# Moving both copies of each sorted tile to ScalarE, and the small loads ahead of the large ones, in a linear-attention and mixture-of-experts kernel

## The chip, the cores and the metric

The kernel runs on one core of a Trainium2 chip. The metric is the device time of one execution in microseconds. Before the change it is 276.43 us, the median of 3 runs that lie between 275.39 and 279.25 us. Engines are named as the profile names them: PE is TensorE (PEld its weight loads), DVE is VectorE, ACT is ScalarE, POOL is GpSimd, SP is SyncE, which here issues the loads.

## The reference

Eight batches of 576 tokens go through a linear attention with 8 heads of 64, and the 4608 rows of 512 that come out go through a mixture of experts in which each token takes its one best expert.

```python
def _attn_ref(q, k, v):                      # (8, 8, 576, 64) each
    q_s = softmax(q, axis=-1)                # over the head dimension
    k_s = softmax(k, axis=2)                 # over the sequence
    kv = np.einsum('bhsd,bhse->bhde', k_s, v)
    return np.einsum('bhsd,bhde->bhse', q_s, kv)

def _moe_ref(x, modality_id, w_gate, modality_bias, w1, w2):   # x (4608, 512)
    logits = x @ w_gate + modality_bias[modality_id]           # 8 experts
    e_idx = np.argmax(logits, axis=1)
    gate_w = softmax(logits)[arange, e_idx]
    for e in range(8):
        mask = e_idx == e
        h = np.maximum(x[mask] @ w1[e], 0.0)                   # 512 -> 1024
        out[mask] = gate_w[mask, None] * (h @ w2[e])           # 1024 -> 512
    return out
```

With the biases of this problem nearly every token goes to one of two experts, one for each modality. The kernel finds these two from the bias table and sorts every batch's tokens by them: tokens of expert A fill the buffer `xs` from the left, those of expert B from the right. It then runs the feed-forward network (FFN) of A over the left part and of B over the right part. A loop at the end serves tokens of other experts. It is skipped if there are none.

## The kernel before

Each batch goes through `prep` (exponentials of k and q on ACT, cast of v), `attend` (attention and gate logits, on PE and DVE) and `route`. `route` picks the expert of each token, builds a permutation `perm` for each of five tiles of tokens (64, then four times 128), scales the attention rows (`scale`), permutes and transposes them on PE (`xT_ps`) and copies each tile into `xs` twice. Copy "a" goes to the left end that expert A has reached, and copy "b" to the right end of B. The rows of the other expert are overwritten by the next tile's copies. Where a copy lands is known only on chip: the copying engine loads the five offsets from `aoff_i` into registers.

```python
        scale(0)
        na = ...; pos = ...                                    # DVE, small
        perm = sb.tile([P, NT, P], BF16, name="perm")
        nc.vector.tensor_tensor(out=perm, in0=iota_row..., in1=pos..., op=ALU.is_equal)
        at = {}
        for side, eng in (("a", ENG.Activation), ("b", ENG.DVE)):
            at[side] = nc.values_load_multi_w_load_instructions(aoff_i[0:1, o : o + NT], engines=[eng], ...)[1]
        yield 3
        scale(1)
        for t in range(NT):
            xT_ps = (ka if b else ff).tile([P, KD, P], FP32, name="xT_ps", ...)
            for kd in range(KD):
                nc.tensor.matmul(out=xT_ps[:, kd, 0:T], lhsT=x_out[t]..., rhs=perm[0:T, t, 0:T], ...)
            if t + 2 < NT:
                xps.append(x_tile(b, t + 2))                   # PE: attention rows of tile t+2
            for side, off, eng in (("a", 0, nc.scalar), ("b", right, nc.vector)):
                a = nc.s_assert_within(at[side][t], ...)
                copy_on(eng, window(a + off, b, T, off > 0), xT_ps[:, :, 0:T], ...)
            yield 1
            if t + 2 < NT:
                scale(t + 2)
```

PSUM pools: `ka` has 2 banks (for `kv_ps`, `tp_ps`, `kvT_ps`, and `xT_ps` after batch 0), `mm` 2 (`x_ps`), `ff` 3 (`h_ps`, `y_ps`), `sp_ps` 1.

The FFN is cut into pieces. One piece of `ffn1` is 8 matmuls of 128x256 into an `h_ps` and a relu on ACT into `hT`; four of them make a pass of 256 tokens. One piece of `ffn2` is 4 matmuls of 128x512 into a `y_ps`, and after every second piece comes the copy to `y_sb` and an indirect store. The copies alternate between DVE and ACT:

```python
            y_sb = ybuf.tile([P, D], FP32, name="y_sb")
            copy_on(nc.scalar if t else nc.vector, y_sb, y_ps)
            store = nc.gpsimd.indirect_dma_start(out=out, ..., in_=y_sb, ...)
```

Instruction order on every engine is fixed by the program: a piece is issued where `weave` calls it. A `yield x` in `attend` or `route` stands for x times `rate` pieces of the FFN of earlier batches:

```python
    def weave(side, rate, preps=(), first=0):
        owed = 0.0
        for i, x in enumerate(side):
            if i >= first:
                next(preps, None)          # ACT exponentials and POOL casts of the next batch
            owed += x * rate
            while owed >= 1:
                mains(1)
                owed -= 1
    ...
    for b in range(2, B):                  # batches 2 to 7
        weave(batch(b), 16 / 24.3, prep(b + 1, nc.gpsimd) if b + 1 < B else (), 4)
```

Batches 0 and 1 are placed by hand ahead of that loop, with the casts of the two experts' weights between them. What is left of the FFN after batch 7 runs at the end, alone. At the start SP issues the loads of batch 0 (k, v, q, 1152 KB each), then the gate weights and the modality ids, then batch 1. The bias table is loaded by POOL's queue. POOL converts the ids (`mbf`) and the gate weights (`wgb`), and POOL and DVE clear two of the four parts of `xs` each.

Of the kernel before, what the change touches and what calls it, by code (L numbers as in the profile page):

```python
# [11 lines left out]
FP32 = mybir.dt.float32  # L12
BF16 = mybir.dt.bfloat16
I32 = mybir.dt.int32
# [6 lines left out]
P = 128  # L21
# [21 lines left out]
def kernel(  # L43
# [67 lines left out]
    def load_batch(b, names="kvq", eng=nc.sync):  # L111
# [13 lines left out]

    load_batch(0)
    bias_1 = const.tile([1, 2, E], FP32)
    nc.gpsimd.dma_start(
        out=bias_1,
# [5 lines left out]
    for hl in range(2):  # L135
# [13 lines left out]
        out=mraw, in_=bass.AP(tensor=m32.tensor, offset=m32.offset, ap=[[2 * S, B], [1, 2 * S]])  # L149
    )  # L150
    load_batch(1)


    ident = const.tile([P, P], BF16)
    make_identity(nc, ident)
# [17 lines left out]
    )  # L173
    iota_i = const.tile([P, E], I32)
    nc.gpsimd.iota(iota_i, pattern=[[1, E]], base=0, channel_multiplier=0)
    wrow = const.tile([P, E], FP32)
# [6 lines left out]
    for hg in range(2):  # L183
# [3 lines left out]
    idh_i = const.tile([P, B, NT], I32)  # L187
    nc.vector.tensor_scalar(out=idh_i, in0=id_i, scalar1=7, scalar2=None, op0=ALU.logical_shift_right)
    idl_i = const.tile([P, B, NT], I32)
    nc.vector.tensor_scalar(out=idl_i, in0=id_i, scalar1=127, scalar2=None, op0=ALU.bitwise_and)  # L190

    vals = const.tile([P, B, NT, 3], BF16)
    nc.vector.tensor_copy(out=vals[:, :, :, 0], in_=idh_i)
    nc.vector.tensor_copy(out=vals[:, :, :, 1], in_=idl_i)

# [15 lines left out]
    mbf = const.tile([B, NJ, 64], BF16)  # L211
    nc.gpsimd.tensor_copy(out=mbf, in_=view(mraw, [[2, NJ], [2 * NJ, 64]]))
    wgb = ybuf.tile([P, D], FP32, name="y_sb").bitcast(BF16)
    nc.gpsimd.tensor_copy(
        out=view(wgb, [[2 * Dh, E], [1, 2 * Dh]], 0, (0, NP)),
# [3 lines left out]
    xs = persist.tile([P, KD, NSLOT], BF16)  # L219
    xs_w = [  # L220
        (nc.vector, nc.gpsimd)[kd % 2].memset(xs[:, kd, :].bitcast(FP32), 0.0) for kd in range(KD)
    ]
    lst = persist.tile([P, 3, NSL], FP32)
# [117 lines left out]

    def copy_on(eng, out, in_, then=lambda w: None):
        then((nc.scalar.copy if eng is nc.scalar else eng.tensor_copy)(out=out, in_=in_))  # L343

# [23 lines left out]
    def attend(b):  # L368
# [58 lines left out]
        nc.scalar.copy(out=kvT, in_=kvT_ps[:, 0 : NP * P])  # L427
        yield 2.3
        g_ps = sp_ps.tile([P, NP, E], FP32, name="g_ps", tag="sp")
# [48 lines left out]

    lws, qis, last_w, ids = {}, {}, {}, {}
    FIRST = [next(x for x in passes if x[0] == ph and x[1] == 0) for ph in range(NPH)]  # L480
# [29 lines left out]
    def route(b):  # L510
# [22 lines left out]
        xps.append(x_tile(b, 1))  # L533
        yield 1.5
        r_ps = sp_ps.tile([P, 2, NT], FP32, name="r_ps", tag="sp")
# [38 lines left out]
        )  # L574
        at = {}
        for side, eng in (("a", ENG.Activation), ("b", ENG.DVE)):
            at[side] = nc.values_load_multi_w_load_instructions(
                aoff_i[0:1, o : o + NT],
                engines=[eng],
                min_val=0,  # L580
                max_val=N - P,
                skip_runtime_bounds_check_because=WHY,
            )[1]
        yield 3
        scale(1)
        for t in range(NT):
            T = tsz[t]
            xT_ps = (ka if b else ff).tile([P, KD, P], FP32, name="xT_ps", tag="ka" if b else "ff")
            for kd in range(KD):
                nc.tensor.matmul(  # L590
                    out=xT_ps[:, kd, 0:T],
                    lhsT=x_out[t][0:T, kd * P : (kd + 1) * P],
                    rhs=perm[0:T, t, 0:T],
                    start=True,
                    stop=True,
                )
            if t + 2 < NT:
                xps.append(x_tile(b, t + 2))
            right = NSLOT - (b * S + cum[t])
            for side, off, eng in (("a", 0, nc.scalar), ("b", right, nc.vector)):  # L600
                a = nc.s_assert_within(at[side][t], 0, b * S + cum[t] - T, skip_runtime_bounds_check_because=WHY)
                copy_on(eng, window(a + off, b, T, off > 0), xT_ps[:, :, 0:T], lambda w: written(w, side))
            yield 1
            if t + 2 < NT:
                scale(t + 2)

        nc.vector.tensor_copy(out=vals[:, b, :, 2], in_=kk)
# [25 lines left out]
        ids[b] = (hlo, hv)  # L633
        yield 1

# [31 lines left out]
    stored = []  # L667

    def ffn1(lo, w, slot, hT):

        nf = 512 // w
        for f0 in range(0, KF, nf):
            h_ps = ff.tile([P, 512], FP32, name="h_ps", tag="ff")
            for f in range(nf):
                for kd in range(KD):
                    nc.tensor.matmul(  # L676
                        out=h_ps[:, f * w : (f + 1) * w],
                        lhsT=W[:, slot, kd * F + (f0 + f) * P : kd * F + (f0 + f + 1) * P],
                        rhs=xs[:, kd, lo : lo + w],
                        start=(kd == 0),  # L680
                        stop=(kd == KD - 1),
                    )
            nc.scalar.activation(  # L683
                out=hT[:, f0 : f0 + nf, 0:w], in_=view(h_ps, [[w, nf], [1, w]]), func=ACT.Relu
            )
            yield

    def ffn2(w, slot, hT, ix, stores):
        for t in range(w // P):
# [11 lines left out]
            y_sb = ybuf.tile([P, D], FP32, name="y_sb")  # L701
            copy_on(nc.scalar if t else nc.vector, y_sb, y_ps)
            store = nc.gpsimd.indirect_dma_start(  # L703
# [31 lines left out]

    def mains(n):
        for _ in range(n):
            next(main, None)
            now[0] += 1

# [13 lines left out]
    def alone(*sides):  # L754
        for side in sides:
            for _ in side:
                pass
# [6 lines left out]
    gating()  # L764
    p0, p1 = prep(0, nc.vector), prep(1, nc.gpsimd)
    alone(p0)
    eids = nc.values_load_multi_w_load_instructions(
# [4 lines left out]
    for b in range(2, B):  # L772
        load_batch(b)
    a0, a1, r0, r1 = attend(0), attend(1), route(0), route(1)
    for _ in range(6):
        next(a0)
    gate_weights()
    next(a0)
    biases()
    next(a0)  # L780
    next(p1)
    next(p1)
    alone(a0)
    next(p1)
    next(p1)
    next(r0)
    next(r0)
    alone(p1)
    cast_weights(0, 0, nc.gpsimd)
    cast_weights(0, 1, nc.scalar)  # L790
    for _ in range(3):
        next(a1)
    next(r0)

    for _ in range(4):
        next(r0)
        next(a1)
    cast_weights(0, 2, nc.gpsimd)
    alone(r0)
    cast_weights(0, 3, nc.scalar)  # L800
    mains(1)
# [9 lines left out]
    cast_weights(1, 2, nc.gpsimd)  # L811
    weave(r1, 0.4)
    cast_weights(1, 3, nc.scalar)
    mains(8 - now[0])
# [15 lines left out]
    for b in range(2, B):  # L830
        weave(batch(b), 16 / 24.3, prep(b + 1, nc.gpsimd) if b + 1 < B else (), 4)
    mains(3)
    places(B - 1)

    cnt = persist.tile([P, 1], FP32)
# [95 lines left out]
```

## Time and profile before

| | |
|---|---|
| median of 3 runs | 276.43 us |
| span of the profiled execution | 278.0 us |
| PE busy | 208.0 us, 75% of the span, 1994 matmuls |
| DVE, ACT, POOL busy | 63%, 46%, 31% |
| loads and stores | 46.58 MB, 168 GB/s over the span |
| first FFN matmul | at 41.99 us |
| batch 2's first attention matmul | at 72.44 us |
| last `xT_ps` matmul, batch 7 | at 219.2 us |
| last store issued | at 266.0 us |

No engine is busy all the time, so the shares alone do not say what bounds the kernel. The useful cut is by stage: the start until the first FFN piece, batch 1 with the first pieces, the six batches of the loop, the rest of the FFN, and the end after the last store. In each one asks what PE waits for, because nearly all the arithmetic is on PE, and at which clock PE ran: the profile gives the granted clock by slice and by window, and the same group of matmuls takes longer where it is low. Times in the profile are of one execution, which was a little longer than the median.

### The profile page before, as it was taken

To read this page: it belongs to the slowest core of one execution; us is meant where nothing else is said; L and a number is where in the kernel's file an instruction comes from. 1 tells how busy PE (TensorE), PEld (TensorE's weight loads), DVE (VectorE), ACT (ScalarE), POOL (GpSimd) and SP (SyncE) were. 2 spreads that over 40 slices of the span, in tenths; PEclk is the share of its full clock that TensorE was granted. 3 is DMA by queue.
4 is the path that set the end of the run, shared out by engine and by line. 5 is a ranking of instruction groups with operands and counts; after the bars stand their busy time and mean duration, and the time that the engine had idled before them with its cause. 6 is when DMAs were issued, how large, how long until landed. Compare 5 with 4: busy or idle time off the path is not lost. (4 is left out here: it accounts for less than half of the span.)

```text
span 278.0 us, 5316 instructions
## 1 busy us (share of the span) xinstructions
PE 208.0 (75%) x1994; PEld 143.7 (52%) x1994; DVE 174.1 (63%) x540; ACT 128.1 (46%) x194; POOL 86.3 (31%) x94
## 2 busy tenths in 40 slices
PE   0075189479997899788878968878897969999910
PEld 0064166246764476465646544646574646666500
DVE  4877886965448677884987778586958761111200
ACT  2333645136974476457638453744152424444200
POOL 6099206014251134151216114320312042222220
PEclk9999999856999799999999999997998899999985
DMA  6999999951999407827731011110012012112200
GB/s 242 369 392 402 398 394 367 365 197 42 361 393 403 168 20 261 325 80 250 254 121 40 38 39 41 40 48 28 2 75 77 2 53 78 73 75 78 93 15 1
DMA packets 19002, 46.58 MB, mean 168 GB/s; under 512 B 1291, under 2 KB 1291, under 8 KB 18972
## 3 DMA queue, kind: packets, MB, share of 16 engines
q1 hardware_dynamic: 15900, 36.76, 36.2%
q0 software_dynamic: 3072, 9.44, 9.0%
q8 instruction: 17, 0.28, 0.4%
q14 instruction: 13, 0.11, 0.1%
HBM read 36.75 MB, written 9.96 MB: 168 GB/s over the span
## 5 line engine op out<-in xcount | busy, mean ns | idle before, releaser
L676 PE MATMUL h_ps<-xs,W 128*128 128x256 bf16 (+1 forms) x640 | 79.7, 278 | 2.7 <-ACT xs L343 2.2
L703 POOL DMA_INDIRECT out_dram<-y_sb,ix x38 | 38.2, 1004 | 132.0 <-DVE y_sb L343 48.3
L692 PE MATMUL y_ps<-W,hT 128*128 128x512 bf16 x304 | 76.8, 391 | 0.0
L676 PEld LDWEIGHTS <-W 128*128 128x128 bf16 x640 | 60.1, 101 | 14.0 <-issue 3.8
L683 ACT ACTIVATE hT<-h_ps 128x512 bf16<-128x512 f32 x76 | 44.7, 599 | 25.2 <-PE h_ps L676 23.0
L692 PEld LDWEIGHTS <-hT 128*128 128x128 bf16 x304 | 27.9, 100 | 27.2 <-issue 3.0
L343 DVE COPY y_sb<-y_ps 128x512 f32<-128x512 f32 x20 | 13.8, 688 | 37.0 <-PE y_ps L692 35.4
L343 ACT CAST xs<-xT_ps 128x512 f32 (+2 forms) x40 | 21.9, 548 | 31.8 <-PE xT_ps L590 31.7
L590 PE MATMUL xT_ps<-perm,x_sb 128*128 128x128 bf16 (+1 forms) x160 | 17.3, 243 | 24.0 <-DVE perm L572 12.9
L343 DVE CAST xs<-xT_ps 128x512 f32 (+2 forms) x40 | 25.5, 637 | 12.8 <-ACT xs L343 12.3
L343 ACT COPY y_sb<-y_ps 128x512 f32<-128x512 f32 x18 | 10.5, 584 | 44.6 <-PE y_ps L692 40.8
L590 PEld LDWEIGHTS <-x_sb 128*128 128x128 bf16 (+1 forms) x160 | 12.3, 111 | 32.3 <-DVE x_sb L558 18.5
L558 DVE TENSOR_TENSOR x_sb<-x_ps,qi 128x512 bf16<-128x512 f32 (+1 forms) x40 | 27.2, 679 | 2.1 <-DVE perm L572 2.1
L623 POOL TENSOR_TENSOR hv<-hhi,vals 128x570 bf16<-128x570 bf16 x8 | 11.8, 1471 | 35.1 <-DVE hhi L619 29.8
L361 ACT ACTIVATE eq<-st 128x1152 bf16<-128x1152 f32 x16 | 18.5, 1165 | 4.5 <-DMA st<-in_q_dram 4.5
L361 ACT ACTIVATE ek<-st 128x1152 bf16<-128x1152 f32 x16 | 18.4, 1164 | 4.2 <-DMA st<-in_k_dram 4.2
L470 PE MATMUL x_ps<-kvbd,et 128*128 128x128 bf16 (+1 forms) x160 | 18.5, 248 | 0.0
L378 PE MATMUL kv_ps<-vb,ek 64*128 64x129 bf16 x288 | 12.6, 239 | 5.3 <-DVE vb L343 2.8
L343 POOL CAST vb<-st 128x1152 bf16<-128x1152 f32 x14 | 15.9, 1159 | 0.0
L378 PEld LDWEIGHTS <-ek 64*128 64x128 bf16 x288 | 10.1, 104 | 8.7 <-issue 7.4
L470 PEld LDWEIGHTS <-et 128*128 128x128 bf16 (+1 forms) x160 | 12.6, 114 | 3.7 <-issue 2.3
L411 PE MATMUL tp_ps<-ident,eq 128*128 128x128 bf16 x144 | 13.8, 242 | 0.5 <-DVE kvbd L399 0.5
(141 smaller groups left out, 212.0 us busy)
## 6 DMA issues: line engine op xcount, KB each, us to landing
st<-in_k_dram SPq DMA_DIRECT2D x8, 1152.0 KB, 7.2
st<-in_v_dram SPq DMA_DIRECT2D x8, 1152.0 KB, 7.9
st<-in_q_dram SPq DMA_DIRECT2D x8, 1152.0 KB, 8.1
st<-in_moe_w_dram SPq DMA_DIRECT2D x8, 1024.0 KB, 11.8
out_dram<-y_sb,ix POOLq DMA_INDIRECT x38, 2.7
W<-in_moe_modality_id_dram SPq DMA_DIRECT2D x1, 36.0 KB
hT<-in_moe_w_gate_dram SPq DMA_DIRECT2D x2, 8.0 KB
bias<-n_moe_modality_bias_dram POOLq DMA_DIRECT2D x1, 0.1 KB, 5.3
```

The costliest lines, as they stand in the source:

```text
L343: then((nc.scalar.copy if eng is nc.scalar else eng.tensor_copy)(out=out, in_=in_))
L361: nc.scalar.activation(out=view((eks if nm == "k" else eqs)[b], [[Dh, 2], [HG * Dh, NJ], [1, Dh]], 2 * g * Dh), in_=src[:, 2 * g : 2 * g + ...
L378: nc.tensor.matmul(out=kv[hg][:, 130 * hp : 130 * hp + 129], lhsT=ek[rows, j, P * hp : P * hp + P], rhs=vb[rows, j, hp, 0:129], start=(j = ...
L411: nc.tensor.transpose(out=view(tp, [[2 * nj * 64, 2], [1, 64]], hp * nj * 64 + jj * 64), in_=eq[:, c0 + jj, P * hp : P * hp + P], identity ...
L470: nc.tensor.matmul(out=view(x_ps, [[2 * Dh, 2], [1, Dh]], (4 * (p_ % 2) + p_ // 2) * Dh, (0, T)), lhsT=et[:, p_, tcol[t] : tcol[t] + T], r ...
L558: nc.vector.tensor_tensor(out=view(x_out[t], [[2 * Dh, HG], [Dh, 2], [1, Dh]], 0, (0, T)), in0=view(xps[t], [[2 * Dh, HG], [Dh, 2], [1, Dh ...
L590: nc.tensor.matmul(out=xT_ps[:, kd, 0:T], lhsT=x_out[t][0:T, kd * P : (kd + 1) * P], rhs=perm[0:T, t, 0:T], start=True, stop=True,)
L623: nc.gpsimd.tensor_tensor(out=hv, in0=view(hhi, [[NSL, NT], [0, 3], [1, NSL]]), in1=view(vals, [[3, NT], [1, 3], [0, NSL]], b * NT * 3), o ...
L676: nc.tensor.matmul(out=h_ps[:, f * w : (f + 1) * w], lhsT=W[:, slot, kd * F + (f0 + f) * P : kd * F + (f0 + f + 1) * P], rhs=xs[:, kd, lo ...
L683: nc.scalar.activation(out=hT[:, f0 : f0 + nf, 0:w], in_=view(h_ps, [[w, nf], [1, w]]), func=ACT.Relu)
L692: nc.tensor.matmul(out=y_ps, lhsT=hT[:, kf, t * P : (t + 1) * P], rhs=W[:, slot, W2 + kf * D : W2 + (kf + 1) * D], start=(kf == 0), stop=( ...
L703: store = nc.gpsimd.indirect_dma_start(out=out, out_offset=bass.IndirectOffsetOnAxis(ap=ix[:, t : t + 1], axis=0), in_=y_sb, in_offset=Non ...
```

## The change

The change has five parts.

1. **Sorted tile.** Both copies of a tile are on ACT. Only ACT loads the five offsets. While the tiles of a batch are sorted, a variable `free` sends relus and output copies that fall there to DVE. Outside, relus and output copies are all on ACT; in the rest of the FFN after the loop the output copies alternate as before.
2. **Small loads first.** Bias table, gate weights and ids are issued by SP ahead of batch 0; the gate weights, the biases and the token ids are made ready before batch 0's attention.
3. **POOL.** It no longer converts ids and gate weights (ACT does), and it clears all of `xs`.
4. **Weight casts.** They are spread anew: ACT casts part 0 of the first expert, DVE part 1, POOL parts 2 and 3; part 3 of the second expert goes from ACT to DVE.
5. **FFN pieces.** The weights of the yields change, above all 3 to 4.5 between `perm` and the first tile, and 1 to 1.4 for each tile, with the rate changed to 16/28.9 so that a batch still has room for 16 pieces. `mains` issues no piece that would need a batch not yet sorted.

The aim is that the chain through a batch's sort no longer alternates between ACT and DVE, that PE has pieces to do where it waited, and that batch 0 gets through sooner.

The diff, cut:

```diff
-    load_batch(0)
     bias_1 = const.tile([1, 2, E], FP32)
-    nc.gpsimd.dma_start(
+    nc.sync.dma_start(
...
+    load_batch(0)
     load_batch(1)
...
-    nc.gpsimd.tensor_copy(out=mbf, ...)
+    nc.scalar.copy(out=mbf, ...)
...
-    nc.gpsimd.tensor_copy(
+    nc.scalar.copy(
         out=view(wgb, ...
...
-    xs_w = [
-        (nc.vector, nc.gpsimd)[kd % 2].memset(xs[:, kd, :].bitcast(FP32), 0.0) for kd in range(KD)
-    ]
+    xs_w = [nc.gpsimd.memset(xs[:, kd, :].bitcast(FP32), 0.0) for kd in range(KD)]
...
         nc.scalar.copy(out=kvT, in_=kvT_ps[:, 0 : NP * P])
-        yield 2.3
+        yield 3
...
-        yield 1.5
+        yield 1.4
...
-        for side, eng in (("a", ENG.Activation), ("b", ENG.DVE)):
-            at[side] = nc.values_load_multi_w_load_instructions(...)[1]
-        yield 3
+        at = nc.values_load_multi_w_load_instructions(..., engines=[ENG.Activation], ...)[1]
+        yield 4.5
         scale(1)
+        free[0] = nc.vector
         for t in range(NT):
...
-            for side, off, eng in (("a", 0, nc.scalar), ("b", right, nc.vector)):
-                a = nc.s_assert_within(at[side][t], ...)
-                copy_on(eng, window(a + off, b, T, off > 0), xT_ps[:, :, 0:T], lambda w: written(w, side))
-            yield 1
+            for side, off in (("a", 0), ("b", right)):
+                a = nc.s_assert_within(at[t], ...)
+                written(nc.scalar.copy(out=window(a + off, b, T, off > 0), in_=xT_ps[:, :, 0:T]), side)
+            yield 1.4
...
+        free[0] = nc.scalar
...
         ids[b] = (hlo, hv)
-        yield 1
+        sorted_.append(b)
+        yield 1.5
...
-            nc.scalar.activation(out=hT..., in_=h_ps..., func=ACT.Relu)
+            if free[0] is nc.vector:
+                nc.vector.tensor_scalar_max(out=h_out, in0=h_in, scalar1=0.0)
+            else:
+                nc.scalar.activation(out=h_out, in_=h_in, func=ACT.Relu)
...
-            copy_on(nc.scalar if t else nc.vector, y_sb, y_ps)
+            copy_on(free[0] or (nc.scalar if t else nc.vector), y_sb, y_ps)
...
         for _ in range(n):
-            next(main, None)
-            now[0] += 1
+            if now[0] < 16 * len(sorted_) - 4:
+                next(main, None)
+                now[0] += 1
...
-    alone(p0)                              # batch 0's exponentials and cast, right after gating()
...
+    gate_weights()
+    biases()
+    token_ids()                            # four small DVE operations, moved from the setup
+    p0, p1 = prep(0, nc.vector), prep(1, nc.gpsimd)
     a0, a1, r0, r1 = attend(0), attend(1), route(0), route(1)
+    alone(p0)
...
-    cast_weights(0, 0, nc.gpsimd)
-    cast_weights(0, 1, nc.scalar)
+    cast_weights(0, 0, nc.scalar)
...
+    cast_weights(0, 2, nc.gpsimd)
+    cast_weights(0, 1, nc.vector)
+    cast_weights(0, 3, nc.gpsimd)
...
-    weave(r1, 0.4)
-    cast_weights(1, 3, nc.scalar)
+    weave(r1, 0.3)
+    cast_weights(1, 3, nc.vector)
...
-        weave(batch(b), 16 / 24.3, ...)
+        weave(batch(b), 16 / 28.9, ...)
     mains(3)
     places(B - 1)
+    free[0] = None
```

## The prediction

> **What bounds the kernel now.** I read the busy time by window first, with borders at the first FFN piece, the first attention matmul of batch 2, the last sorted tile and the last store. Columns: window, length, busy time of each engine (instructions), granted PE clock, DMA share, GB/s.
>
> ```profile
> 0.00:42.00 42.00, 16.90 (x200) 13.84 (x201) 32.37 (x97) 17.68 (x21) 19.37 (x34) 1.00 0.98 366
> 42.00:72.40 30.40, 23.13 (x172) 15.76 (x171) 20.49 (x61) 13.90 (x21) 11.35 (x8) 0.78 0.71 250
> 72.40:219.50 147.10, 124.77 (x1308) 86.23 (x1308) 108.77 (x333) 79.91 (x126) 40.37 (x37) 0.97 0.38 138
> 219.50:265.80 46.30, 43.24 (x318) 27.83 (x315) 12.48 (x51) 16.65 (x28) 14.25 (x14) 1.00 0.18 68
> 265.80:278.00 12.20, 0.00 (x0) 0.00 (x0) 0.00 (x0) 0.00 (x0) 0.97 (x1) 0.61 0.03 9
> ```
>
> The first stage belongs to no engine: a chain through loads, DVE and ACT. In the loop PE is busy 124.8 of 147.1 us, DVE 74%, ACT 54%, so PE is the nearest bound and its 22.3 us of idle time are what can be had. In the rest PE is nearly full. Next, PE's list of waits in the loop's window (who waited for whom, us in total, times, longest):
>
> ```profile
> PE xT_ps L590 <- DVE x_sb L558: 8.3, 10, 1.3
> PE xT_ps L590 <- DVE perm L572: 5.2, 6, 1.2
> PE g_ps L431 <- ACT kvT L427: 2.9, 5, 0.8
> PE kv_ps L378 <- DVE xs L343: 2.5, 5, 0.6
> PE h_ps L676 <- ACT xs L343: 1.3, 1, 1.3
> PE kvT_ps L425 <- ACT et L343: 0.8, 5, 0.2
> PE r_ps L536 <- DVE isa L528: 0.6, 1, 0.6
> PE tp_ps L411 <- DVE kvbd L399: 0.5, 1, 0.5
> ```
>
> These are 22.1 us, all of PE's idle time in the loop, and three quarters stand in the sort. Third, the timeline of one sort, batch 6 (DVE):
>
> ```profile
> 160.75 0.82 DVE L572 TENSOR_TENSOR perm<-iota_row,pos 128x640 bf16<-128x640 bf16 x1
> 162.38 0.69 DVE L558 TENSOR_TENSOR x_sb<-x_ps,qi 128x512 bf16<-128x512 f32 x1 [0.80 <-DVE perm L572]
> 162.99 0.41 DVE L343 CAST xs<-xT_ps 128x256 f32 x1
> 163.32 0.68 DVE L558 TENSOR_TENSOR x_sb<-x_ps,qi 128x512 bf16<-128x512 f32 x1
> 164.24 0.69 DVE L343 CAST xs<-xT_ps 128x512 f32 x1 [0.24 <-ACT xs L343]
> ```
>
> After `perm` DVE stands 0.80 us before `scale(1)`; in program order only its load of five offsets lies there. Then scales and "b" copies alternate. A "b" copy waits for the "a" copy of ACT, though both only read `xT_ps`.
>
> **What the Trainium skill says.** (1) "PSUM — Partial Sum Buffer", section "PSUM bank collisions raise a hardware error": two engines may not touch one bank and partition at once, reads included. The trace agrees: in all, 12.3 us (21 times) of DVE's idle time before `xs` copies end with ACT's `xs` copy. So copies on two engines do not run side by side; moving "b" to ACT lengthens no tile. (2) "TensorE: Matmul & The Clock Gate", section "What's actually happening": the PE clock is halved after an idle spell, and activity restores it. The trace agrees in kind: granted clock 0.50 from 56 to 65 us, after a wait of 3.15 us; there 4 FFN matmuls take 1.91 us, at full clock 1.03. (3) "SBUF — State Buffer", section "Who interferes with whom": a DVE instruction with two SBUF inputs is held up by a GpSimd one that reads SBUF. The trace agrees: `perm` of batch 0 beside a POOL weight cast takes 2.46 us, the median 0.83.
>
> ```profile
> 30.98 1.90 POOL L343 CAST W<-st 128x2048 bf16<-128x2048 f32 x1 [3.57 <-DMA st<-in_moe_w_dram]
> 31.09 2.46 DVE L572 TENSOR_TENSOR perm<-iota_row,pos 128x640 bf16<-128x640 bf16 x1
> ```
>
> **Part by part.**
>
> *The loop, engines.* Per batch DVE loses five "b" copies: 4 x 0.69 + 0.42 = 3.2 us (rows by shape), and the 0.8 us at the offsets. ACT gains the same copies at its own rate: 4 x 0.59 + 0.37 = 2.7 us. In the program's order per batch two output copies fall into the sort, so they stay two on DVE and two on ACT, and nearly all 8 relus stay on ACT. ACT per batch: exponentials 4 x 1.16 = 4.7, et 1.0, kvT 0.6, relus 8 x 0.6 = 4.8, outputs 2 x 0.58 = 1.2, copies 2 x 2.7 = 5.5, sum 17.8, with the offset load about 19 us. DVE: 108.8 / 6 = 18.1 - 3.2 = 15 us. PE: in the loop 124.8 us, less about 2 for part of the slow clock (3% of it is 3.7), so 20.5 us. PE stays the bound, ACT comes close.
>
> *The loop, PE's waits.* For `perm`: between `r_ps` and the first tile most batches had 2 pieces and have 3 now. A piece is 0.9 us (timeline of the rest, full clock: four ffn1 pieces, 32 matmuls, take 3.66 us, four ffn2 pieces, 16 matmuls, 3.62), the wait 0.7 to 1.2. I leave 0.5 of 5.2. For `x_sb`: `scale(1)` comes 0.8 us sooner, a piece stands before the second tile, and no scale queues behind a copy; 1 of 8.3. For `kvT`: two pieces instead of one before `g_ps`; 0.5 of 2.9. `kv_ps` waited for the last "b" copy; now ACT has finished both under one or two pieces; 0 of 2.5. `h_ps` before its batch is sorted: the new limit in `mains` excludes it; 0 of 1.3. `kvT_ps` and `r_ps` stay, 1.4. New loss: between `kv_ps` and `tp_ps` one piece stands now where there were often two, while `kinv` and `kvbd` take 0.23 + 0.18 + 1.2 = 1.6 us and the two `ka` banks are held: 0.8 x 6 = 5. Sum 8.4 us, and I add 3 for waits on a fuller ACT: 11.4 instead of 22.3.
>
> The program's order also puts 92 pieces between batch 2's start and the last tile, before 89: 2.7 us more there, and 4 fewer (3.6 us) in the rest. The loop: 122.8 + 2.7 + 11.4 = 137 instead of 147.
>
> *The start.* Loads of batch 0 are issued later by the SP time of the small ones: 1.49 for gate weights (x2), 0.42 ids, about 0.4 bias: 2.3 us. So k lands near 8.8 (before, ACT began at 6.40), q near 15.4 (13.08). In return DVE is free when v lands near 12; before it began that cast at 13.32, at the end of the gating chain, and each half took 1.73 us beside POOL. I take PE's `kv_ps` as done at 17.5 (18.0), then the exponentials of q as the limit, `kvT` near 20; `g_ps` then finds gate weights and biases done, and `gx` ends near 20.5, not 23.45. From there to `perm` took 10.1 us; without the slowed `lg` addition (1.25 instead of 0.20) and `perm` (2.46, 0.83) it is 7.5, so 28 to 29. ACT must cast weight part 0 before its copies; that part follows batch 1 in the queue and lands near 27, so the first copy is near 29.5. DVE's cast of part 1 (1.2 us) stands in the sort. The first FFN piece comes at 37, before 42.
>
> *Batch 1.* Its wait for `perm` (3.15 us) and the half clock after it stay, since one piece and a DVE weight cast are still all that stands there. One piece more (0.9), a shorter sort, less of POOL: 29.5 instead of 30.4.
>
> *The rest:* 46.3 - 3.6 = 42.7. *The end:* 12.2, untouched.
>
> Sum: 37 + 29.5 + 137 + 42.7 + 12.2 = 258.4 against a span of 278.0. The median lies 1.6 under the span, hence **257 us**.
>
> **The rivals.** *ACT becomes the bound.* 19 of 22 us is 86%, in order: the relus of three pieces stand behind the offset load (ACT already waited 1.14 us there in batch 7), then ten copies of 5.5 us. If PE waits 2 us more per batch, on relus or `xT_ps` banks, the loop gives back 12 us and the time is 269. Against it: exponentials fall outside the sort, and PE's own work within it is about 7 us. *The start is lost to the loads.* If batch 0 is bound by its loads, 2.3 us late, the first piece comes at 41 to 44, and the time is 261 to 264. For it: DMA is at 0.98 over the first 42 us. Against it: after q lands PE still needed 20 us to the first tile, all in DVE, ACT and POOL. *The clock.* If fuller PE stays at full clock after 60 us, about 4 us more are saved: 253. If the gap in batch 1 lengthens, half clock spreads.
>
> **Range and chances.** The mechanism of the sort is measured wait by wait, so I hold a gain of at least 8 us likely. The first two rivals together would make 272 or so, the good clock with no unseen waits 250. Range 248 to 268. Faster by over 2% (under 270.9): 0.88; within 2%: 0.09; slower: 0.03.
>
> **What would show it.** First FFN matmul near 37 us. PE's waits for `x_sb` and `perm` in the loop under 2 us together, and a new one, `tp_ps` for `kvbd`, near 5. No DVE gap after `perm`. ACT near 18 us a batch. PE's idle time in the loop halved. The prediction is wrong if PE's waits move to `hT` or to ACT's `xs` copies, if the first tile is not sorted before 33 us, or if the window from 42 to 72 us gains or loses more than 3 us.

## The result and the profile after

The changed kernel takes **261.2 us** (258.62 to 263.39) against 276.19 us (275.39 to 279.25) before: ratio 0.9402, 95% interval 0.9311 to 0.9492. The prediction was 257.0, range 248 to 268. Two further measurements of the same kernel, on other chips, gave 0.9667 (0.9639 to 0.9695) and 0.9506 (0.9441 to 0.9571); what is known of the difference stands with the first experiment.

The busy time by window, with the borders at the same events as before (first FFN piece, batch 2's first attention matmul, last sorted tile), the last one now at the last FFN matmul, which gave before a rest of 45.6 us. Columns: window, length, busy time of PE, PE's weight loads, DVE, ACT, POOL (instructions), granted PE clock, DMA share, GB/s. This profiled execution took 258.62 us. Ratios in this document leave out executions more than 1.5% above the quickest of their kernel; the profiled execution before, with 279.76 us, is such a one, and the one after is the quickest of its four, so these two lie 21 us apart and the medians 15.0.

```profile
0.00:38.00 38.00, 15.70 (x194) 13.24 (x194) 30.53 (x94) 22.06 (x26) 18.07 (x33) 1.00 0.92 346
38.00:65.35 27.35, 19.74 (x186) 14.45 (x186) 21.00 (x54) 13.55 (x26) 11.47 (x8) 0.88 0.88 325
65.35:202.96 137.61, 121.54 (x1319) 83.87 (x1319) 90.69 (x306) 92.41 (x157) 42.01 (x39) 1.00 0.43 155
202.96:244.36 41.40, 39.97 (x300) 25.98 (x297) 9.64 (x47) 15.96 (x27) 13.27 (x14) 1.00 0.20 76
244.36:257.00 12.64, 0.00 (x0) 0.00 (x0) 0.69 (x1) 0.00 (x0) 1.22 (x2) 0.63 0.03 9
```

The span fell by 21.0 us: 4 in the start (42.0 to 38.0), 3 in batch 1, 9.3 in the loop (146.9 with this border, now 137.6), 4.2 in the rest. A part of this, some 6 us in all, belongs to the two executions and not to the change. In the loop, for one, PE's list of waits fell by 6.3 us (22.1 to 15.8), and PE's busy time by 3.0 (124.5 to 121.5) at a granted clock of 1.00 instead of 0.97. There DVE and ACT are now equally loaded, 91 and 92 us. PE's list of waits in the loop's window says what its 16 us of idle time are now (who waited for whom: us in total, times, longest):

```profile
PE r_ps L537 <- DVE isa L529: 7.3, 6, 1.6
PE tp_ps L412 <- DVE kvbd L400: 3.2, 6, 0.7
PE xT_ps L590 <- DVE x_sb L559: 2.6, 6, 1.2
PE xT_ps L590 <- DVE perm L573: 1.0, 6, 0.2
PE kvT_ps L426 <- ACT et L344: 0.8, 5, 0.2
PE h_ps L680 <- ACT xs L602: 0.7, 1, 0.7
```

The two rows that were largest, `x_sb` at 8.3 and `perm` at 5.2, are 2.6 and 1.0; `kvT` and `kv_ps` have left the top. In their place stands a row that was 0.6: PE waits for `isa`, the selection out of the gating logits, before the rank sums `r_ps`. The timeline of DVE in one sort (batch 4; start, duration) shows what became of the gap after `perm`:

```profile
127.21 0.82 DVE L573 TENSOR_TENSOR perm<-iota_row,pos 128x640 bf16<-128x640 bf16 x1
127.95 0.68 DVE L559 TENSOR_TENSOR x_sb<-x_ps,qi 128x512 bf16<-128x512 f32 x1
128.55 0.16 DVE L657 TENSOR_SCALAR ix<-sel 128x2 int32<-128x2 f32 x1
128.72 0.69 DVE L559 TENSOR_TENSOR x_sb<-x_ps,qi 128x512 bf16<-128x512 f32 x1
```

`scale(1)` follows `perm` at once, where it stood 0.80 us behind it, and no copy stands between two scales.

### The profile page after: what moved, and what is told of

Same layout as the page of the kernel before. It is cut to its first block, busy times and chain, and to the rows that moved or that the text cites. A ratio compares the mean times of both kernels' runs of the same rounds, so it can differ in the third digit from the quotient of the medians.

```text
span 257.0 us, 5305 instructions
## 1 busy us (share of the span) xinstructions
PE 196.9 (77%) x1994; PEld 137.5 (54%) x1994; DVE 152.6 (59%) x500; ACT 144.0 (56%) x234; POOL 86.0 (33%) x93
## 3 DMA queue, kind: packets, MB, share of 16 engines
q1 hardware_dynamic: 15902, 36.76, 39.2%
## 5 line engine op out<-in xcount | busy, mean ns | idle before, releaser
L709 POOL DMA_INDIRECT out_dram<-y_sb,ix x38 | 37.6, 990 | 134.9 <-DVE y_sb L344 49.4
L680 PE MATMUL h_ps<-xs,W 128*128 128x256 bf16 (+1 forms) x640 | 74.4, 267 | 2.3 <-ACT xs L602 2.3
L698 PE MATMUL y_ps<-W,hT 128*128 128x512 bf16 x304 | 74.6, 382 | 0.0
L680 PEld LDWEIGHTS <-W 128*128 128x128 bf16 x640 | 57.6, 98 | 11.9 <-issue 2.9
L691 ACT ACTIVATE hT<-h_ps 128x512 bf16<-128x512 f32 x75 | 43.5, 598 | 32.5 <-PE h_ps L680 24.6
L602 ACT CAST xs<-xT_ps 128x512 f32 (+2 forms) x80 | 38.7, 565 | 15.7 <-PE xT_ps L590 14.1
L698 PEld LDWEIGHTS <-hT 128*128 128x128 bf16 x304 | 27.5, 98 | 25.7 <-issue 1.9
L590 PE MATMUL xT_ps<-perm,x_sb 128*128 128x128 bf16 (+1 forms) x160 | 15.8, 224 | 13.5 <-DVE perm L573 9.4
L344 POOL CAST vb<-st 128x1152 bf16<-128x1152 f32 x14 | 17.0, 1218 | 8.4 <-DMA st<-in_v_dram 8.4
L471 PE MATMUL x_ps<-kvbd,et 128*128 128x128 bf16 (+1 forms) x160 | 17.3, 237 | 0.0
L412 PE MATMUL tp_ps<-ident,eq 128*128 128x128 bf16 x144 | 13.5, 241 | 3.2 <-DVE kvbd L400 3.2
L412 PEld LDWEIGHTS <-eq 128*128 128x128 bf16 x144 | 10.9, 110 | 5.8 <-DVE kvbd L400 4.4
L344 DVE COPY et<-tp_ps 128x1024 bf16<-128x1024 bf16 (+1 forms) x16 | 7.7, 489 | 8.1 <-PE tp_ps L412 7.6
```

The source lines that it names most:

```text
L412: nc.tensor.transpose(out=view(tp, [[2 * nj * 64, 2], [1, 64]], hp * nj * 64 + jj * 64), in_=eq[:, c0 + jj, P * hp : P * hp + P], identity ...
L471: nc.tensor.matmul(out=view(x_ps, [[2 * Dh, 2], [1, Dh]], (4 * (p_ % 2) + p_ // 2) * Dh, (0, T)), lhsT=et[:, p_, tcol[t] : tcol[t] + T], r ...
L590: nc.tensor.matmul(out=xT_ps[:, kd, 0:T], lhsT=x_out[t][0:T, kd * P : (kd + 1) * P], rhs=perm[0:T, t, 0:T], start=True, stop=True,)
L602: written(nc.scalar.copy(out=window(a + off, b, T, off > 0), in_=xT_ps[:, :, 0:T]), side)
L680: nc.tensor.matmul(out=h_ps[:, f * w : (f + 1) * w], lhsT=W[:, slot, kd * F + (f0 + f) * P : kd * F + (f0 + f + 1) * P], rhs=xs[:, kd, lo ...
L691: nc.scalar.activation(out=h_out, in_=h_in, func=ACT.Relu)
```

## The experiments

Theory: the gain is the end of the alternation between ACT and DVE in the sort (part 1), plus an earlier first tile (parts 2 to 4); the placement of pieces (part 5) chooses where PE waits. Rivals: the pieces carry it; or the start does. The runs stand in three groups, each beside the kernel before on one chip, and are best compared within their group. Group 2 has no unaltered changed kernel.

| group | kernel | us | ratio to before (interval) |
|---|---|---|---|
| 1 | all parts | 265.32 | 0.9667 (0.9639 to 0.9695) |
| 1 | without part 1's copies | 274.58 | 0.9955 (0.9923 to 0.9986) |
| 1 | without part 5 | 265.57 | 0.9687 (0.9622 to 0.9751) |
| 1 | without parts 2 to 4 | 262.92 | 0.9577 (0.9549 to 0.9605) |
| 2 | all parts, nothing sent to DVE | 261.44 | 0.9394 (0.9304 to 0.9484) |
| 2 | part 1 alone | 264.64 | 0.9548 (0.9494 to 0.9602) |
| 2 | part 5 alone | 268.11 | 0.9676 (0.962 to 0.9732) |
| 2 | all, later casts | 261.01 | 0.9408 (0.9339 to 0.9478) |
| 3 | all parts | 263.24 | 0.9506 (0.9441 to 0.9571) |
| 3 | all, clearing of `xs` later | 265.04 | 0.9573 (0.9493 to 0.9653) |
| 3 | all, one piece shifted | 262.28 | 0.9439 (0.9351 to 0.9526) |
| 3 | all, with the three edits together | 262.73 | 0.9495 (0.9415 to 0.9575) |

**The changed kernel again** (group 1; no edit).

> The changed kernel once more, as the measure for the runs beside it. Expected 259 to 263 us and, in its profile, the loop from 65 to 203 us with about 15 us of PE waits, as in the profile already seen.

It took 265.32 us, and not 261. Its stages differ from the first profile's in batch 1 (29.0 instead of 27.35, at a granted clock of 0.82 instead of 0.88) and in the loop (142.4 instead of 137.6). In the loop 1.6 us are PE's busy time (123.1, 121.5), and 3.2 are one row of the waits, 7.3 in the first profile:

```profile
PE r_ps L537 <- DVE isa L529: 10.5, 6, 1.8
```

Behind it stands that DVE begins later on the gating logits. The timeline of PE and DVE, first in the changed kernel's first profile (the bracket is DVE's idle time before, and its releaser):

```profile
120.86 0.66 PE L441 MATMUL lg_ps<-gx,et 128*128 128x18 bf16 x20
...
121.37 1.02 PE L698 MATMUL y_ps<-W,hT 128*128 128x512 bf16 x4
121.55 0.20 DVE L450 TENSOR_SCALAR qi<-lg_ps 128x40 f32<-128x40 f32 x1 [0.98 <-PE lg_ps L441]
```

and in this run:

```profile
124.47 0.66 PE L441 MATMUL lg_ps<-gx,et 128*128 128x18 bf16 x20
...
124.98 1.02 PE L698 MATMUL y_ps<-W,hT 128*128 128x512 bf16 x4
125.79 0.20 DVE L450 TENSOR_SCALAR qi<-lg_ps 128x40 f32<-128x40 f32 x1 [1.61 <-PE lg_ps L441]
```

Same program, same PE schedule, but DVE starts 1.32 instead of 0.69 us after the first of the `lg_ps` matmuls. The semaphore updates in the trace say more: PE's update for `lg_ps` comes 0.67 us after its first matmul in the one and 1.30 in the other, and DVE starts 0.02 us after it in both. So it is PE's signal that is late, and not DVE. The difference reappears in the wait of `r_ps` for `isa`, 1.76 instead of 1.14 us a batch, and a steady batch takes 23.98 instead of 23.36 us. This late start is there in some executions and not in others, from batch 2 or 3 on. It was late in the profiles of group 1's first, second and fourth kernels and all of group 3, and early in those of before and of group 2. What decides it stays open; the chip alone does not, since the third kernel of group 1 ran on the same chip and was mostly early. It is worth about 0.62 x 6 = 3.7 us, an estimate. It is known for the profiled executions only, so a difference of that size between two medians says nothing by itself.

**The sort's copies back on two engines** (group 1; parts 2 to 5 stay).

```diff
-        at = nc.values_load_multi_w_load_instructions(..., engines=[ENG.Activation], ...)[1]
+        for side, eng in (("a", ENG.Activation), ("b", ENG.DVE)):
+            at[side] = nc.values_load_multi_w_load_instructions(..., engines=[eng], ...)[1]
...
-        free[0] = nc.vector
...
-            for side, off in (("a", 0), ("b", right)):
+            for side, off, eng in (("a", 0, nc.scalar), ("b", right, nc.vector)):
...
-        free[0] = nc.scalar
```

> Part 1 undone in the changed kernel: copy b on DVE again, offsets loaded on both engines, relus on ACT, output copies alternating; start and pieces stay new. Theory A (taking DVE out of the tile chain is what removed PE's waits for x_sb and perm): the waits for x_sb come back to 6 us or more in the loop, the 0.8 us gap of DVE after perm comes back, time 267 to 271. Rival B (the new placement of the pieces alone covers these waits): x_sb stays under 3 us, time 260 to 264.

It took 274.58 against 265.32 with the copies on ACT, and both profiled executions have the late start: 9.3 us lost. (Theory A's 267 to 271 was meant beside a changed kernel at 261.) In the profiles 1.4 us of it lie in the start, 3.0 in batch 1 and 5.6 in the loop. Of the 5.6, PE's waits make 2.6 and its busy time 3.0 (126.1, 123.1, both at a clock of 0.99). PE's largest waits in the loop, and DVE's wait for ACT's copies:

```profile
PE r_ps L537 <- DVE isa L529: 10.4, 6, 2.0
PE xT_ps L591 <- DVE x_sb L559: 5.7, 12, 0.8
PE tp_ps L412 <- DVE kvbd L400: 2.9, 6, 0.5
DVE xs L604 <- ACT xs L604: 4.5, 12, 0.6
```

`x_sb` is back, at 5.7 us twelve times (2.6 with the copies on ACT). DVE's wait for ACT's copy of the same tile is back too. Before the change it was

```profile
DVE xs L343 <- ACT xs L343: 9.0, 16, 1.3
```

and in the changed kernel, where DVE copies no tile, there is none. DVE's gap after `perm` is 0.46 us again in most batches, where 0.8 was expected. This run gives DVE back the copies, the waits for ACT, the offset load and 16 us of work in the loop (107.0, 90.7) all at once. No run parts them, with both copies on DVE for instance, so how much the hand-overs cost by themselves is not shown. From the first tile to the next batch's first matmul, batch 4's sort takes 7.65 us, with both copies on ACT 6.71.

**The pieces back** (group 1).

```diff
-        yield 3
+        yield 2.3
...
-        yield 4.5
+        yield 3
...
-        weave(batch(b), 16 / 28.9, ...)
+        weave(batch(b), 16 / 24.3, ...)
```

(and the other yields, the rate in batch 1 and the limit in `mains`, as before the change)

> Part 5 undone in the changed kernel: yields, rates and mains as before the change; sort on ACT and new start stay. Theory A: PE's waits for x_sb in the loop stay under 4 us, those for perm return to about 5, kvT to 3, while r_ps for isa (7.3 us now) falls to about 1; the sum of waits is 15 to 18 us and the time 261 to 265. Rival B: all waits return, 20 us or more, time 268 to 272.

It took 265.57 us, the same as all parts in this group. But its profiled execution mostly had the early start, where the changed kernel takes about 261. If the others had it too, which is not known, part 5 is worth some 4 us here, an estimate. In its loop list the old names of the waits come back, and the row for `isa` is gone:

```profile
PE xT_ps L590 <- DVE perm L573: 4.6, 6, 1.1
PE xT_ps L590 <- DVE x_sb L559: 3.7, 5, 1.2
PE g_ps L432 <- ACT kvT L428: 2.9, 5, 0.8
```

**The start back** (group 1: parts 2 to 4 undone).

```diff
+    load_batch(0)
     bias_1 = const.tile([1, 2, E], FP32)
-    nc.sync.dma_start(
+    nc.gpsimd.dma_start(
...
-    gate_weights()
-    biases()
-    token_ids()
...
```

> Parts 2, 3 and 4 undone: loads, POOL's work, token ids and weight casts as before the change; sort and pieces stay new. If the stages add, the loop stays as in the changed kernel and the first FFN piece comes at 41 to 43 us instead of 38: time 264 to 267. If the earlier start is worth nothing because batch 1 and its weights set the start of the loop anyway: the loop starts at 65 to 66 us all the same and the time is 260 to 263.

With these parts undone the median is 2.4 us *lower*: 262.92 against 265.32, with intervals that don't meet. Both profiled executions have the late start and the same time, 264.94 and 264.84 us; but the first is the slowest of its five, the others take 262.78 to 263.06, and whether they had the late start is not known. So the parts are not shown to cost anything, and they are not shown to gain anything either. In the profiles the first FFN piece comes at 41.26 us instead of 37.75, but batch 2 begins only 1.2 us later (67.98, 66.75). Most of the head start is lost inside batch 1. Here are DVE and POOL there, first in the changed kernel of this group:

```profile
49.88 2.46 DVE L543 TENSOR_TENSOR qi<-qi,gsum 128x40 f32<-128x40 f32 x1
50.38 1.90 POOL L344 CAST W<-st 128x2048 bf16<-128x2048 f32 x1
...
54.64 0.37 PE L590 MATMUL xT_ps<-perm,x_sb 64*128 64x64 bf16 x4 [5.41 <-DVE perm L573]
```

then with the start undone:

```profile
43.88 1.89 POOL L343 CAST W<-st 128x2048 bf16<-128x2048 f32 x1
...
52.20 0.20 DVE L542 TENSOR_TENSOR qi<-qi,gsum 128x40 f32<-128x40 f32 x1
...
54.71 0.27 PE L589 MATMUL xT_ps<-perm,x_sb 64*128 64x64 bf16 x4 [3.15 <-DVE perm L572]
```

With the old start POOL's weight cast is over before batch 1's gating; with the new one it falls beside DVE's small multiplication of two SBUF operands, which takes 2.46 us instead of 0.20. Those 2.26 us are the difference between a wait of 5.41 and one of 3.15, and as much as batch 1 loses (3.5 us of head start become 1.2). That they are the cause is not shown: the later casts below take the collision away and batch 1 gets no shorter. A rival is the clock, granted at 0.94 in batch 1 with the old start and at 0.82 with the new. The two profiled spans are equal, 263.3 us: the head start of 1.2 us at batch 2 is gone by the end of the loop.

**Relus and outputs not sent to DVE** (group 2).

```diff
-        free[0] = nc.vector
...
-        free[0] = nc.scalar
```

> The changed kernel with half of part 1 undone: both copies of a tile stay on ACT, but relus stay on ACT and output copies alternate as before the change, also inside the sort. If the two copies on ACT carry part 1: time within 2 us of the changed kernel (ratio 0.965 to 0.972), PE's wait for x_sb in the loop 2 to 4 us. If it is the freeing of ACT by DVE: PE waits for hT or for ACT's xs copies and at least half of part 1's 9 us is lost, ratio 0.98 or more.

The ratio is 0.9394, as quick as the changed kernel on its own chip (0.9402) and as the last kernel of this group, which sends relus and outputs to DVE and has 0.9408. This half of part 1 does nothing measurable; the copies, with their offset load, carry it.

**Part 1 alone, and part 5 alone** (group 2). The first is the kernel before with only the hunks of part 1 (copies, offsets, `free`), the second with only the yields, the limit and the rates of part 5, as the front's diff shows them.

> The kernel before with part 1 alone (both copies on ACT, relus and outputs of the sort on DVE); start and pieces as before. Theory A (part 1 carries the gain, the rest adds nothing in sum): ratio 0.96 to 0.972. If the parts only work together: 0.98 to 1.0.

> The kernel before with the new placement of the pieces alone. Theory A: no gain, ratio 0.99 to 1.005: the waits for perm and kvT shrink and one for isa takes their place, while x_sb stays near 8 us. If the placement is worth what the prediction gave it: 0.965 to 0.98.

Against 277.3 us before on this chip, part 1 alone gains 12.7 us and part 5 alone 9.2; all together but for the sending to DVE, in the same group and also with the early start, 15.9. I had expected nothing of part 5. The stages (us):

| kernel | start | batch 1 | loop | rest |
|---|---|---|---|---|
| before | 42.0 | 30.4 | 146.9 | 45.6 |
| part 1 alone | 43.0 | 25.1 | 136.5 | 45.8 |
| part 5 alone | 40.1 | 29.1 | 143.2 | 41.2 |
| all, nothing to DVE | 37.6 | 31.1 | 137.2 | 41.1 |
| all, later casts | 39.2 | 27.5 | 138.9 | 41.4 |

Part 1 alone takes the loop down by 10.4 against the profile of before, of which 4.5 are PE's busy time (124.5, 120.0); adding the other parts doesn't shorten the loop further. Part 5 shortens the *rest* by 4.4: it is 41.1 to 41.4 in every kernel that has part 5, and 45.6, 45.8 or 43.7 (with the new start) in those that have not. It puts FFN pieces into the loop's gaps, so that fewer are left at the end. The loop then does more at the same length. Waits in the loop, part 1 alone, then part 5 alone:

```profile
PE xT_ps L589 <- DVE perm L572: 4.1, 6, 0.7
PE g_ps L431 <- ACT kvT L427: 3.4, 5, 0.8
```

```profile
PE r_ps L536 <- DVE isa L528: 6.8, 6, 1.1
PE xT_ps L590 <- DVE x_sb L558: 5.5, 11, 0.9
```

The wait for `isa` belongs to part 5, the one for `x_sb` to the absence of part 1. The two gains overlap, for 12.7 and 9.2 are more than 15.9; that both fill the same gaps in the sort is a reading of these lists and not tested by itself.

**Later casts of the second weight slot** (group 2): they stand behind batch 1's first step instead of ahead of it.

```diff
-    cast_weights(1, 1, nc.vector)
-    cast_weights(1, 2, nc.gpsimd)
-    weave(r1, 0.3)
+    weave(r1_casts(), 0.3)     # yields r1's first step, issues both casts, then the rest of r1
```

> The changed kernel with two weight casts of the second expert (part 1 on DVE, part 2 on POOL) issued after the first sorted tile of batch 1 instead of ahead of its perm. If the earlier start was lost there (perm of batch 1 waited for by PE 5.4 us, with 1.22 us of a DVE cast and a multiplication of 2.46 us beside POOL's cast in the chain): that wait falls to 2 us or less, the loop starts 2.5 to 4 us sooner, near 63 to 64 us, ratio 0.95 to 0.96. If the DMA of the weights or batch 2 sets the start of the loop: unchanged, 0.965 to 0.97.

Here the multiplication takes 0.20 us again, but the wait for `perm` is still 4.3, where 2 or less was expected, and the ratio is 0.9408, no gain. Batch 1 takes 27.5 us, against 27.35 in the first profile; and in group 3, the kernel with all three edits, this one among them, has a batch 1 of 29.5 us, and the one with the later clearing alone 29.2. So the slow multiplication isn't what the head start was lost to, or something else takes its place. The profile also shows a loss in the first 17 us, ahead of anything that this edit touches: a one-row cast of DVE took 8.52 us beside POOL's clearing of `xs`, so that the cast of v began at 16.84 us instead of 15.30, and the first FFN piece at 39.19 instead of 38.00. The next edit goes there.

**The changed kernel as control, and clearing `xs` later** (group 3): DVE and POOL share the clearing, after the gating's small copies.

```diff
-    xs_w = [nc.gpsimd.memset(xs[:, kd, :].bitcast(FP32), 0.0) for kd in range(KD)]
...
+        for kd in range(KD):      # at the end of the copies to krow; POOL's first waits for them
+            xs_w.append((nc.vector, nc.gpsimd)[kd % 2].memset(xs[:, kd, :].bitcast(FP32), 0.0))
```

> The changed kernel once more, unaltered, as the measure for the three runs beside it. Two executions of it differed by 6 us: in the quicker one VectorE began on lg_ps 0.69 us after its first matmul (a steady batch of 23.36 us), in the other 1.33 us after it (23.98 us). Either may come: 261 us with the early start, 265 us with the late one.

> The changed kernel, with the clearing of xs shared between VectorE and GpSimd and set after the gating. Theory (GpSimd's 8.36 us of memsets hold up the start of VectorE's chain, whose one-row cast took 4.25 us, and so the cast of v, which began at 15.3 us): that cast starts at 12 to 13 us, the first FFN piece near 36.5 instead of 38 us, and the whole is 1 to 1.5 us shorter. Rival (the casts of q and the first gather bound the start): the v cast moves, the first FFN piece stays at 38 and the time too. Second rival: it is given back in batch 1, as the 4 us of the start parts were: the first FFN piece moves and the start of batch 2 doesn't.

The control took 263.24 us; its profiled execution has the late start in the loop. The timeline of the start in the changed kernel:

```profile
4.68 4.25 DVE L264 CAST parts<-left 1x16 bf16<-1x16 f32 x1
...
4.73 8.36 POOL L223 MEMSET xs<- 128x2432 f32 x4
...
15.30 1.42 DVE L344 CAST vb<-st 128x1152 bf16<-128x1152 f32 x2
```

and with `xs` cleared later:

```profile
4.68 0.26 DVE L264 CAST parts<-left 1x16 bf16<-1x16 f32 x1
...
13.27 1.42 DVE L354 CAST vb<-st 128x1152 bf16<-128x1152 f32 x2
...
30.21 1.23 DVE L354 CAST W<-st 128x2048 bf16<-128x2048 f32 x1 [0.87 <-DMA st<-in_moe_w_dram]
```

A cast of 16 numbers takes 0.26 us, not 4.25, once no clearing by POOL stands beside it. (The Trainium skill, page "SBUF — State Buffer", section "Who interferes with whom": a DVE cast can enter a mode in which DVE and GpSimd exclude each other for whole instructions. The trace agrees in kind: 4.25 us is two of the four memsets of 2.09.) The cast of v begins 2.0 us sooner, batch 0's `perm` 1.2 us sooner (27.91, 29.11), and the first FFN piece 0.4 us sooner (37.61, 38.00): now the casts of the first expert's weights wait for their load, as the last line shows. The time, 0.9573 against 0.9506, is no better. The outcome is the first rival's, but by another cause than it named: not the casts of q and the first gather, but the load of the weights takes over.

**One piece shifted** (group 3), from behind the first sorted tile to the place between the logits and the rank sums.

```diff
-        yield 2.3
+        yield 3.7
...
-            yield 1.4
+            yield 1.4 if t else 0
```

> The changed kernel with one FFN piece of each batch taken from behind the first sorted tile and put between the gating logits and the rank sums. Theory (PE waits 7.3 us for VectorE's isa there only because too few pieces lie between lg_ps and r_ps; a piece is 1.0 us and the wait 1.14 us a batch): the wait for isa falls to 1 or 2 us in the loop, the one for perm stays under 1.5, and the time falls by 4 to 5 us. Rival (the sum of the chain lg to perm to x_sb is fixed, and a piece moved ahead is a piece missing behind): the wait for isa falls by 6 us and those for perm and x_sb rise by as much, and the time stays within 1 us.

```profile
PE r_ps L537 <- DVE isa L529: 5.3, 6, 1.0
PE tp_ps L412 <- DVE kvbd L400: 3.2, 6, 0.7
PE xT_ps L590 <- ACT xs L602: 2.3, 5, 1.2
PE xT_ps L590 <- DVE perm L573: 1.1, 6, 0.2
```

This profiled execution has the late start, as that of the control beside it, whose row for `isa` is 10.5. The piece takes 5.2 us off that row, not all of it (with the early start 0.63 us a batch less would remain, an estimate); of the freed time 2.3 turn up as a new wait for ACT's `xs` copies, while `x_sb` falls from 2.6 to 0.3. A steady batch takes 23.63 us against 23.97 in the control, and the profiled execution 262.76 us against 265.82. The times, 262.28 (0.9439) and 263.24 (0.9506), have intervals that overlap. The loop is 3.5 us shorter in the profiles (138.8, 142.3), of which steady batches make 0.34 x 6 = 2 us, and batch 1 is 0.6 longer. So the edit moves the waits as the theory says, but the medians are 1 us apart, and it isn't shown to be faster.

**The three edits together** (group 3).

> The changed kernel with three edits: the clearing of xs after the gating, the casts of the second weight slot set after batch 1's first step, and the FFN piece shifted ahead of the rank sums. If the three are worth what their theories say, the gains add up (1 from the start, 1 from batch 1, 4 from the loop): 255 us, quicker than both kernels. If the waits only change their names, it is within 1.5 us of the changed kernel.

It took 262.73 us, a ratio of 0.9495, within the control's interval: the gains don't add up to 255. The wait for `isa` is 5.3 us here too, and the one for ACT's `xs` copies 2.3. In this group no kernel is shown to beat the changed one.

## Why the prediction was right, step by step

The mechanism in the sort was right and its size about right: undone it costs 9.3 us, alone it gives 12.7. The gain as a whole was put at 19.4 us and is 15.0, so the median of 261.2 lies 4.2 above the prediction. That the sum of 258.4 us for the span met 257.0 in the first profile is partly luck: this is the quickest execution of four, and in the loop two errors of 4 us cancel.

- *Start, 37:* measured 38.0. One term was off: I had DVE free for v "when v lands near 12", but POOL's memsets held its chain, the cast began at 15.30, and `gx` ended at 22.4, not 20.5. From there to the end of `perm` it took 7.5 us, as in the sum. The step that failed is what the 4 us are worth: with the old start batch 2 begins 1.2 us later by the profiles, and the time is no worse. Of the start's predicted 5 us none is shown to be left at the end.
- *Batch 1, 29.5:* 27.35 in the first profile, 29.0 and 29.3 in the others. "Its wait for `perm` (3.15 us) stays": it grew to 5.41, as DVE's multiplication beside POOL's cast grew by 2.26. With part 1 and the old start the stage takes 25.1 and 26.7 us, at a granted clock of 0.93 and 0.94, where it was 0.78 before; how much of that is the shorter sort and how much the clock is open.
- *Loop, 137:* 137.6 in the first profile, but 142.3 and 142.4 with the late start. PE's own work was 121.5, not the 125.5 that I summed; the third rival (a full clock, 1.00 instead of 0.97) came true in the loop of this execution. Waits were 15.8, not 11.4.
- *Waits by name:* `perm` 1.0 (I said 0.5), `x_sb` 2.6 (1), `kv_ps` 0.2 (0), `tp_ps` 3.2 (5). The term that failed is `r_ps`, left at about 0.6: it is 7.3. I counted pieces in front of the tiles and did not count those between `lg_ps` and `r_ps`, where two of four were taken away: in a steady batch PE's order there has four pieces before the change and two after, and the run with part 5 alone, which has the same order, waits 6.8. The 3 us "for waits on a fuller ACT" weren't there: ACT's only new row is 0.7, before `h_ps`. ("Three quarters stand in the sort" holds with the rows that wait for `xs` copies; `x_sb` and `perm` alone were 13.5 of the 22.1 us.)
- *Engines:* DVE 90.7 / 6 = 15.1 us a batch (15). ACT 92.4 / 6 = 15.4 us, against 18: copies issued back to back overlap, so that ten of them take 4.6 us a batch and not 5.5, and there were 46 relus and 22 exponentials in the loop where I had 48 and 24; the rest of the difference isn't traced. So the first rival, ACT as the bound, did not come, nor did PE's waits move to `hT`.
- *Rest, 42.7:* 41.4; its PE work fell from 43.4 to 40.0 us.
- *The second rival*, the start lost to the loads, is half true. The first piece comes early, and most of the gain is then lost in batch 1, by a cause that stays open; weight loads bound the start only where the chain is made quicker still.
- *The signs that I named:* the first tile before 33 us (its two copies end at 31.1) and no DVE gap after `perm` came true. But `x_sb` and `perm` are 3.6 us together and not under 2, PE's idle time in the loop fell from 22.3 to 16.1 us and did not halve, and the window of batch 1 lost 3.05 us, just past the 3 that I had set as a sign of being wrong.

## What to carry to other kernels

Where two engines take turns on one PSUM tile, look for waits of the one for the other (9.0 us of DVE's here), try both copies on one engine, and check by undoing it alone; here that was worth 9.3 us, with the relief of the other engine in it. Pieces that fill a PE wait must be counted stage by stage along the whole chain, since each one placed in one gap is missing in another, and what they buy may show in the tail, as the 4.4 us here. An earlier start is worth only what reaches the next stage: read the borders of the following stages before counting it.

## What the runs showed of the hardware

PE's semaphore update for `lg_ps` comes either 0.66 to 0.74 us behind the first matmul of the group or 1.02 to 1.53 (mostly about 1.30), in the same program with the same PE schedule, and DVE follows mostly 0.02 us behind it; the cause is open. A cast of 1x16 values on DVE took 4.25 us in the first profile and 8.52 in another execution whose program is the same up to there, about two and four of POOL's memsets of 2.09, and 0.26 with the memsets placed later. ACT's copies of 128x512 take 0.59 us one by one, and six of them in a row 3.04 us.
